# A planned attention-then-mixer kernel: the first pair's squares on ACT, the third group's squares planned later, by-token products spread among MLP tiles

## The chip, the cores and the metric

One core of one Trainium2 chip runs the whole program. The metric is the device time in microseconds (us). In the rounds here every timed run lies within 0.3% of its kernel's median; every comparison is of runs made in turn on the same chip. Engines: PE is the tensor engine, ACT the scalar engine, DVE the vector engine, POOL is GpSimd, SP the sync engine.

## The reference, cut to what matters

```python
# q, k, v: (8, 12, 448, 64) float32; U: (448, 32); V: (32, 448); w_ch1: (768, 3072); w_ch2: (3072, 768)
def _attn_ref(q, k, v, tau):
    q_n = q / (norm(q, axis=-1) + 1e-6)
    k_n = k / (norm(k, axis=-1) + 1e-6)
    attn = softmax(q_n @ k_n.T / tau)
    return attn @ v

def _moe_ref(x, U, V, w_ch1, w_ch2):          # x: the attention output as (8, 448, 768)
    u = x + ((x.T @ U) @ V).T                 # the low-rank mixer over tokens
    return u + relu(u @ w_ch1) @ w_ch2        # the MLP
```

## The kernel before

Every instruction is an `Op`; a planner written in Python simulates the engines with estimated durations, fixes the order on every engine, and the kernel then issues that order. ACT, DVE and PE run their queues in the order fixed, so an instruction that waits holds all behind it: in the traces below ACT stood 1.14 us ahead of a waiting square with an exponential ready behind it (before, 10.62). A `prio` says which of several ready instructions an engine takes (small first), `hold` and `deps` say what must be done before.

Heads go in pairs (two heads), pairs' statistics in groups: the first group is pair 1, the second pair 2, the third pairs 3 and 4, the fourth pairs 5 and 6. For each pair: squares, sums, ln and exp for the norm, products to normalise the rows (`xn`), transposes on PE (`tp`), scores (`sc`), exponentials on ACT, products with attention's V (`av`).

```python
def squares(b, g, ld, ops, lo, ii, ss, pr, on, hold):
    for i in ii:                                   # 0 is q, 1 is k
        for a0 in range(0, g, G // 2):
            o = Op(on, ..., deps=[ops[i], *hold], acq=[sq], prio=pr + 0.2, fast=True)   # x * x
            red.append(plan.add(Op("DVE", ..., deps=[o], ...)))                         # reduce_sum
# ... (cut)
def stats_first(ld, ops):
    for i in range(2):
        done[i], up = scales(0, 0, 2, ld, ops, 0, (i,), inv, -1 - 0.1 * i, ("DVE", "ACT")[i])
# ... (cut)
def by_tokens(us, A, X):                           # batch 0: u = x + A V, six products
    for i in range(3):
        for c0, c1 in ((0, CH), (CH, C)):
            mm = Slot(r_mm, 1)                     # one of three PSUM buffers
            o = plan.add(Op("PE", ...matmul(mm, V_sb[...], A[:, c0:c1])), pe_mlp)
            plan.add(Op("DVE", ...tensor_add(us[i][:, c0:c1], mm, X[:, i, c0:c1]), deps=[o], rel=[mm, X]))
# ... (cut)
for f in range(NC):                                # mlp: 24 tiles of relu(u @ w_ch1)
    if b == 0 and f == 9:
        by_tokens(us, *state["first"])
# ... (cut)
z = fill(lambda: nc.vector.memset(V_sb, 0.0), 500, prio=-1.3)
first = ...                                        # loads of q, k of pair 1, by SP
second = load_qk(0, 2, 4, uses=2)                  # the other loads, by POOL
ld, ops, _ = load_qk(0, 4, 8)
id_set = plan.add(Op("POOL", 0.8, lambda: make_identity(nc, ident)), pool_q)
begun = stats_first(*first[:2])
stats(0, 2, 4, *second, hold=begun)
zf = fill(lambda: nc.vector.memset(U_f(), 0.0), 400, prio=0.1, acq=[uv], deps=begun)
u0, v0, u1 = ...                                   # loads of the mixer's U and V, by SP, behind zf
stats(0, 4, 8, ld, ops, 0, hold=got[0, 0, "qkT"][2])   # third group: behind the copies of pair 1's transposes
load_v0()                                          # attention's V of batch 0, eight loads by POOL
ld, ops, _ = load_qk(0, 8, 12)
late = stats(0, 8, 12, ld, ops, 0)                 # fourth group
# ... (cut)
consts = [POOL cast of U, POOL cast of V into V_sb, POOL cast of U]
```

Of the kernel before, what the change touches and what calls it, by code (L numbers as in the profile page):

```python
# [49 lines left out]
class Plan:  # L50
# [52 lines left out]
    def run(self):  # L103
# [22 lines left out]
        while left:  # L126
# [6 lines left out]
            while progress:  # L133
                progress = False
                for e in self.ENGINES:
                    if free[e] > t + 1e-9:
                        continue
                    pick = None
                    if e in heads:
                        for k, s in enumerate(self.streams[e]):  # L140
                            i = heads[e][k]
                            if i < len(s):
                                r = self.ready_at(s[i], e)
                                if r is None:
                                    continue
                                if r <= t + 1e-9:
                                    pick = s[i]
                                    heads[e][k] += 1
                                    break
                                heapq.heappush(events, r)  # L150
                    else:
                        w = known[e]
                        for i, (_, _, o) in enumerate(w):
                            if o.start is not None:
                                continue
                            if e == "ACT" and o.fast and free["DVE"] <= t + 1e-9:
                                continue
                            r = self.ready_at(o, e)
                            if r is None:
                                continue  # L160
                            if r <= t + 1e-9:
                                pick = o
                                break
                            heapq.heappush(events, r)
                            if r <= t + self.HOLD:
                                break
                        if pick is not None:
                            del w[i]
                    if pick is None:
                        continue  # L170
                    o = pick
                    o.start, o.by = t, e
                    o.end = t + (o.dur[e] if isinstance(o.dur, dict) else o.dur)
                    free[e] = o.end
                    o.end += self.LAG[e]
                    if isinstance(o.lat, tuple):
                        q, work, fixed = o.lat
                        dma[q] = max(dma[q], o.end) + work
                        o.end = dma[q] + fixed
                    else:  # L180
                        o.end += o.lat
                    for s in o.acq:
                        if s.i is None:
                            s.i = s.ring.n
                            s.ring.n += 1
                    for s in o.rel:
                        s.left -= 1
                        s.last = max(s.last, o.end)
                        if s.left == 0:
                            s.ring.freed[s.i] = s.last  # L190
                    for c in kids.pop(o.seq, ()):
                        waits[c.seq] -= 1
                        if waits[c.seq] == 0:
                            offer(c)
                    order.append(o)
                    left -= 1
                    progress = True
                    heapq.heappush(events, free[e])
                    heapq.heappush(events, o.end + self.SEM)
# [5 lines left out]
def kernel(  # L205
# [12 lines left out]
    nc = tc.nc  # L218
# [276 lines left out]
    def stats_first(ld, ops):  # L495

        inv = Slot(r_inv, 3)
        done, ups = {}, []
        for i in range(2):
            done[i], up = scales(0, 0, 2, ld, ops, 0, (i,), inv, -1 - 0.1 * i, ("DVE", "ACT")[i])  # L500
            ups.append(up)
        return ups + norm(0, 0, ld, 0, inv, 0, done, -1)

# [58 lines left out]
    def attention(b, p, X):  # L562
# [4 lines left out]
        for m in (0, 1, 2, 6, 3, 4, 5) if b == 0 else range(7):  # L567
            sc = Slot(r_sc, 1)

            def score(sc=sc, m=m):  # L570
# [7 lines left out]
                out=attn.tile[:, m, off:off + S], in_=sc.tile[:, 0:S], func=AF.Exp,  # L578
                scale=inv_tau), deps=[o], acq=[attn], rel=[sc], prio=0.1 if b == 0 else 1))
        last_exp[b] = exps[5]  # L580
        muls = []
        for hh in range(2):
            h = 2 * p + hh
# [138 lines left out]
        prev["A"], prev["X"] = A, X  # L722
        return us, uT, ut

    def by_tokens(us, A, X):

        for i in range(3):
            for c0, c1 in ((0, CH), (CH, C)):
                mm = Slot(r_mm, 1)
                o = plan.add(Op("PE", pe_t(CH), lambda i=i, c0=c0, c1=c1, mm=mm: nc.tensor.matmul(  # L730
                    out=mm.tile[:, 0:CH], lhsT=V_sb[:, PAD + 128 * i:PAD + 128 * i + 128],
                    rhs=A.tile[:, c0:c1], start=True, stop=True), acq=[mm, us[i]], rel=[A]), pe_mlp)
                got.setdefault((0, "u"), []).append(plan.add(Op(
                    "DVE", dve_t(CH), lambda i=i, c0=c0, c1=c1, mm=mm: nc.vector.tensor_add(  # L734
                        out=us[i].tile[:, c0:c1], in0=mm.tile[:, 0:CH], in1=X.tile[:, i, c0:c1]),
                    deps=[o], rel=[mm, X], prio=2)))


    def mlp(b, us, uT, ut):
# [28 lines left out]
        for f in range(NC):  # L768
            if f % AHEAD == 0:
                for g in range(f, f + AHEAD):  # L770
                    early[g] = Slot(r_sc if b == 0 and f == 0 else r_mm, 1)
                    if f == 0 and b == 0:
                        up(g, early[g], range(CC - 1))
            if b == 0 and f == 9:
                by_tokens(us, *state["first"])
            mm = early[f]
            o = up(f, mm, range(CC - 1, CC) if b == 0 and f < AHEAD else range(CC))
            r = Op("ACT/DVE", any_t(n), None, deps=[o], acq=[relu], rel=[mm],
# [65 lines left out]
        nc.vector.memset(t_[96:128, :, 0:PAD].bitcast(mybir.dt.uint32), ones)  # L844

    attn_set = [fill(lambda t_=t_: set_attn(t_), 1000, prio=i - 2.5) for i, t_ in enumerate(attn_t)]
    z = fill(lambda: nc.vector.memset(V_sb, 0.0), 500, prio=-1.3)

    def load_u(par):
        off = PAD * par  # L850
# [25 lines left out]
    state, last_mul = {}, []  # L876

    def att(b):
        X = Slot(r_X, 0)
        muls = []  # L880
        for p in range(NPAIR):
            muls += attention(b, p, X)
        last_mul.extend(muls)
        return stage0(b, X, muls)
# [2 lines left out]
        out=lead.tile[:, i], in_=src[0, 0:2].rearrange("h (s c) d -> s h (c d)", c=SC)),  # L887
        acq=[uv], prio=-5, lat=2.5)) for i, src in enumerate((q, k))]
    second = load_qk(0, 2, 4, uses=2)
    ld, ops, _ = load_qk(0, 4, 8)  # L890
    id_set = plan.add(Op("POOL", 0.8, lambda: make_identity(nc, ident)), pool_q)
    begun = stats_first(*first[:2])
    stats(0, 2, 4, *second, hold=begun)
    xn_set.append(fill(lambda: nc.vector.memset(xn_t[2][:, 0:8, :], 0.0), 900, prio=0.2, deps=begun))
    zf = fill(lambda: nc.vector.memset(U_f(), 0.0), 400, prio=0.1, acq=[uv], deps=begun)
    u0 = load_u(0)
    v0 = [plan.add(Op("SP", 0.45, lambda t=t: nc.sync.dma_start(out=V_f()[R * t:R * (t + 1)], in_=moe_V),
                      deps=[zf, *begun], prio=-2, lat=12.0)) for t in range(4)]
    u1 = load_u(1)
    stats(0, 4, 8, ld, ops, 0, hold=got[0, 0, "qkT"][2])  # L900
    load_v0()
    ld, ops, _ = load_qk(0, 8, 12)
    late = stats(0, 8, 12, ld, ops, 0)
    load_w1(0, 6)
    load_w1(6, 12)
    v_set = [fill(lambda: set_v(v_t[0]), 1000, prio=-1.4),
             fill(lambda: set_v(v_t[1]), 1000, prio=3, deps=late)]
    consts = [plan.add(Op("POOL", 0.4, lambda: cast_u(0), deps=u0 + [z], rel=[uv]), pool_q),
              plan.add(Op("POOL", 1.2, cast_v, deps=v0 + [z], rel=[uv]), pool_q),
              plan.add(Op("POOL", 0.4, lambda: cast_u(1), deps=u1 + [z], rel=[uv]), pool_q)]  # L910
# [67 lines left out]
```

## Time and profile before

| | before |
|---|---|
| time, median of three runs | 604.51 us (604.49 to 605.16) |
| span of the profiled run | 603.2 us |
| first transposes on PE | 7.62 us |
| first exponential on ACT | 11.16 us |
| attention's V landed for the first head | 14.61 us |
| transposes of the second pair | 15.39 us |
| first scores of the third pair | 22.27 us |
| first full MLP tile | 41.29 us |

Times of events are from the span's start. In a timeline a line gives start, length, engine, line of the program, operation, tiles and count, and in brackets how long the engine had been idle and what ended that. The prediction below shows the lines that carry its argument. Two stretches matter later and are not in it. The first is DVE between 15 and 18 us, where before the copy of the second pair's transposed q stood in the midst of other work:

```profile
15.08 0.68 DVE L461 TENSOR_REDUCE ss<-sq 112x8 f32<-112x512 bf16 x1
16.36 0.75 DVE L826 COPY qkT<-tp 128x672 bf16<-128x672 bf16 x3 [0.60 <-PE tp L374]
17.03 0.68 DVE L461 TENSOR_REDUCE ss<-sq 112x8 f32<-112x512 bf16 x1
```

DVE waited 0.60 us for PE there. A table by stretch gives start and end, length, busy time of PE, weight loads, DVE, ACT and POOL with counts, then PE's clock, the DMA share and GB/s.

```profile
21.20:24.60 3.40, 1.99 (x18) 1.04 (x15) 3.30 (x11) 3.40 (x12) 1.16 (x1) 1.00 1.28 213
```

PE is busy for 1.99 of 3.40 us here.

One caution on every clock shown below, and in the prediction's table. The clock records of a trace begin late, here at 17.77 us, and the views show 1.00 for all that comes earlier. The products tell otherwise. The eight transposes at 15.39 (0.94 us, in the prediction) are 93 to 94 ns apart from start to start after the second (the first two 75), those at 19.79 are 48 to 51 ns apart:

```profile
19.79 0.56 PE L374 MATMUL tp<-ident,xn 112*128 112x112 bf16 x8
```

So PE ran at about half its clock at 15.39. A clock share below tells only of a fall after the first record.

### The profile page before, as it was taken

What the parts mean: (1) busy time and instruction counts of PE and PEld (TensorE: products, weight loads), DVE (VectorE), ACT (ScalarE), POOL (GpSimd) and SP (SyncE); (2) the same over time, 40 slices, a digit from 0 to 9 for tenths busy, and PEclk for the clock granted to TensorE, in tenths of its full rate; (3) what the DMA queues carried; (4) which work ended last, traced back from release to release, by engine and by line L of the source; (5) the groups of instructions that cost most, each with busy time, mean ns of one, the idle gap of its engine ahead of it and who ended that gap; (6) DMA issues with size and microseconds to landing.
All of it is one profiled execution on the core that took longest, in us unless ns stands there. A gap on an engine that the chain in (4) does not pass through costs nothing.

```text
span 603.2 us, 11528 instructions
## 1 busy us (share of the span) xinstructions
PE 586.4 (97%) x4725; PEld 347.0 (58%) x4725; DVE 300.6 (50%) x728; ACT 276.9 (46%) x598; POOL 115.2 (19%) x175
## 2 busy tenths in 40 slices
PE   3899999999999999999999999999999999999997
PEld 1565666555565665666445666566545666654565
DVE  8979749989999988554731244014300210110011
ACT  5877652488874277316741067505642025014300
POOL 8246334062706116000600000000000000000000
PEclk9999999999999999999999999999999999999999
DMA  9999999999999959725922133030002110310021
GB/s 144 193 188 112 204 201 107 150 173 136 159 152 155 149 102 154 95 57 90 123 29 66 52 74 47 1 93 27 15 1 53 52 40 1 90 42 1 0 53 54
DMA packets 150165, 54.81 MB, mean 91 GB/s; under 512 B 115040, under 2 KB 150112, under 8 KB 150112
## 3 DMA queue, kind: packets, MB, share of 16 engines
q0 software_dynamic: 72864, 25.73, 38.4%
q1 hardware_dynamic: 77184, 28.32, 24.4%
q8 instruction: 37, 0.61, 0.4%
q14 instruction: 16, 0.13, 0.1%
q10 hardware_dynamic: 64, 0.02, 0.0%
HBM read 52.25 MB, written 11.01 MB: 105 GB/s over the span
## 4 chain that ended last, share of the span: by engine, by line
PE 93%; DVE 2%; ACT 2%; POOL 1%; DMA 1%; issue 0%; ACTq 0%; POOLq 0%
PE mm L794 36%; PE mm L760 35%; PE sc L572 10%; PE av L592 8%; PE mm L684 1%; PE tp L374 1%; DMA v_nat<-in_v_dram 1%; DVE xn L536 1%; PE mm L649 1%; POOL v_nat L429 1%; ACT attn L577 1%; PE sc L760 0%; POOL qk_nat L396 0%; DVE ss L461 0%; ACT qkT L824 0%
## 5 line engine op out<-in xcount | busy, mean ns | idle before, releaser
L760 PE MATMUL mm<-uT,w_sb 128*128 128x512 bf16 (+1 forms) x1134 | 241.3, 353 | 0.2 <-DVE u_nat L734 0.2
L794 PE MATMUL mm<-w_sb,relu 128*128 128x384 bf16 (+1 forms) x1368 | 231.3, 323 | 0.0
L577 ACT ACTIVATE attn<-sc 128x448 bf16<-128x448 f32 x336 | 164.6, 552 | 110.9 <-PE av L592 58.2
L794 PEld LDWEIGHTS <-relu 128*128 128x128 bf16 x1368 | 132.7, 98 | 86.1 <-issue 0.2
L760 PEld LDWEIGHTS <-w_sb 128*128 128x128 bf16 x1152 | 111.8, 98 | 102.7 <-issue 1.8
L783 ACT ACTIVATE relu<-mm 128x512 bf16<-128x512 f32 (+1 forms) x158 | 86.8, 549 | 129.3 <-PE mm L760 128.7
L803 DVE TENSOR_TENSOR O_sb<-mm,u_nat 128x384 f32<-128x384 f32 (+1 forms) x57 | 31.2, 549 | 210.8 <-PE mm L794 207.4
L572 PE MATMUL sc<-qkT 128*128 128x448 bf16 x336 | 102.7, 356 | 3.7 <-ACT attn L577 2.0
L592 PEld LDWEIGHTS <-attn 128*128 128x128 bf16 x1536 | 62.1, 98 | 17.8 <-issue 2.5
L418 POOL DMA_DIRECT2D v_nat<-in_v_dram x98 | 63.2, 655 | 31.7 <-DMA w_sb<-in_moe_w_ch_dram 15.8
L592 PE MATMUL av<-v_nat,attn 128*128 128x65 bf16 x1536 | 66.6, 194 | 0.8 <-DMA v_nat<-in_v_dram 0.4
L461 DVE TENSOR_REDUCE ss<-sq 112x8 f32<-112x512 bf16 x96 | 63.1, 673 | 0.2
L536 DVE TENSOR_TENSOR xn<-qk_nat,inv 112x512 bf16<-112x512 bf16 x94 | 60.9, 681 | 2.4 <-DMA qkT<-xn 2.2
L396 POOL DMA_DIRECT2D qk_nat<-in_q_dram x24 | 17.2, 718 | 136.5 <-DVE xn L536 117.0
L572 PEld LDWEIGHTS <-qkT 128*128 128x128 bf16 x336 | 28.9, 98 | 22.1 <-issue 7.3
L601 DVE TENSOR_TENSOR X_sb<-av,rd 128x256 bf16<-128x256 f32 x96 | 40.1, 419 | 1.6
L599 DVE RECIPROCAL rd<-av 128x4 f32<-128x4 f32 x96 | 17.1, 179 | 37.6 <-PE av L592 36.9
L457 DVE TENSOR_TENSOR sq<-qk_nat 112x512 bf16<-112x512 bf16 x87 | 33.7, 415 | 0.0
L698 DVE TENSOR_TENSOR u_nat<-mm,X_sb 128x384 bf16<-128x384 f32 x36 | 19.2, 553 | 15.4 <-PE mm L684 15.1
L785 DVE TENSOR_SCALAR relu<-mm 128x384 bf16<-128x384 f32 (+1 forms) x31 | 18.7, 604 | 12.8 <-PE mm L760 12.0
L374 PE MATMUL tp<-ident,xn 112*128 112x112 bf16 x144 | 11.9, 226 | 7.8 <-DVE xn L536 7.6
L474 ACT ACTIVATE ln<-ss 112x32 f32<-112x32 f32 (+2 forms) x26 | 6.0, 231 | 27.3 <-DVE ss L461 27.1
(61 smaller groups left out, 172.5 us busy)
## 6 DMA issues: line engine op xcount, KB each, us to landing
qk_nat<-in_q_dram POOLq DMA_DIRECT2D x23, 224.0 KB, 5.2
qk_nat<-in_k_dram POOLq DMA_DIRECT2D x23, 224.0 KB, 6.3
w_sb<-in_moe_w_ch_dram POOLq DMA_DIRECT2D x4, 1152.0 KB, 14.6
w_sb<-in_moe_w_ch_dram POOLq DMA_DIRECT2D x8, 576.0 KB, 15.8
out_dram<-O_sb SPq DMA_DIRECT2D x15, 168.0 KB, 2.2
out_dram<-O_sb SPq DMA_DIRECT2D x16, 144.0 KB, 2.1
out_dram<-O_sb SPq DMA_DIRECT2D x16, 120.0 KB, 2.0
out_dram<-O_sb SPq DMA_DIRECT2D x16, 96.0 KB, 2.2
```

Of the source, the lines that this page charges most:

```text
L418: nc.gpsimd.dma_start(out=vb[p0:p0 + s1 - s0, hs, j, 0:D], in_=v[b, hs].rearrange("h (s c) d -> c s h d", c=SC)[c, s0:s1]),
L457: nc.vector.tensor_mul(y, x, x)
L461: lambda i=i, a0=a0, a1=a1, sq=sq: nc.vector.reduce_sum(ss.tile[:, i, a0:a1, :].rearrange("p h c -> p (h c)"), sq.tile[:, 0:a1 - a0, :].re ...
L536: nc.vector.tensor_mul(dst, src, sc)
L572: nc.tensor.matmul(out=sc.tile[:, 0:S], lhsT=kT[:, 128 * m:128 * (m + 1)], rhs=qkT.tile[:, 8:12, :].rearrange("p c s -> p (c s)"), start=T ...
L577: exps[m] = plan.add(Op("ACT", act_t(S), lambda sc=sc, m=m: nc.scalar.activation(out=attn.tile[:, m, off:off + S], in_=sc.tile[:, 0:S], fu ...
L592: nc.tensor.matmul(out=av.tile[:, t, 0:D + 1], lhsT=attn.tile[:, m, 128 * t:128 * (t + 1)], rhs=v_t[b % 2][:, h, j, 0:D + 1], start=(j == ...
L601: muls.append(plan.add(Op("DVE", dve_t(256), lambda av=av, rd=rd, h=h: nc.vector.tensor_mul(X.tile[:, :, h * D:(h + 1) * D], av.tile[:, :, ...
L760: o = plan.add(Op("PE", pe_t(n), lambda cc=cc: nc.tensor.matmul(out=mm.tile[:, 0:n], lhsT=w1_sb[:, cc, f * 128:(f + 1) * 128], rhs=uT.tile ...
L783: nc.scalar.activation(out=relu.tile[:, f, 0:n], in_=mm.tile[:, 0:n], func=AF.Relu)
L794: nc.tensor.matmul(out=mm.tile[:, 0:c1 - c0], lhsT=relu.tile[:, f, i * 128:(i + 1) * 128], rhs=w2_t[:, f, c0:c1], start=(f == 0), stop=(f ...
L803: nc.vector.tensor_add(out=O.tile[:, 0:w], in0=mm.tile[:, 0:w], in1=us[i].tile[:, c0:c1]),
```

## The change

The intent: start the first pair sooner by giving both of its squares to ACT, which is free (idle 2.26 us ahead of its first square in the trace before), and clearing the mixer's `V_sb` later; let the first exponentials run before the third group's squares; and spread the six by-token products of batch 0, which hold PE behind each other's adds, one by one among MLP tiles.

```diff
-                            if e == "ACT" and o.fast and free["DVE"] <= t + 1e-9:
+                            if e == "ACT" and o.fast and "/" in o.eng and free["DVE"] <= t + 1e-9:
-            done[i], up = scales(0, 0, 2, ld, ops, 0, (i,), inv, -1 - 0.1 * i, ("DVE", "ACT")[i])
+            done[i], up = scales(0, 0, 2, ld, ops, 0, (i,), inv, -1 - 0.1 * i, "ACT")
+        if b == 0 and p == 0:
+            last_exp["first"] = [exps[1]]
-    def by_tokens(us, A, X):
+    def by_tokens(us, A, X, part):
     ... (cut: one product per call)
-            if b == 0 and f == 9:
-                by_tokens(us, *state["first"])
+            if b == 0 and 9 <= f < 21 and f % 2:
+                by_tokens(us, *state["first"], (f - 9) // 2)
-    z = fill(lambda: nc.vector.memset(V_sb, 0.0), 500, prio=-1.3)
+    z = fill(lambda: nc.vector.memset(V_sb, 0.0), 500, prio=3, deps=begun)
+    muls0 = attention(0, 0, X0)                      # pair 1 entered into the plan here
-    stats(0, 4, 8, ld, ops, 0, hold=got[0, 0, "qkT"][2])
+    stats(0, 4, 8, *third, hold=last_exp["first"])
     ... (cut: the same loads entered earlier, in the same order on POOL)
```

More of the change, by code (lines that the diff above doesn't have):

```diff
@@ L723, in stage0 @@
         return us, uT, ut
-    def by_tokens(us, A, X):
-        for i in range(3):
-            for c0, c1 in ((0, CH), (CH, C)):
+    def by_tokens(us, A, X, part):
+        for i in range(part // 2, part // 2 + 1):
+            for c0, c1 in [((0, CH), (CH, C))[part % 2]]:
                 mm = Slot(r_mm, 1)
@@ L878, in att @@
     def att(b):
-        X = Slot(r_X, 0)
-        muls = []
-        for p in range(NPAIR):
+        X = Slot(r_X, 0) if b else X0
+        muls = [] if b else list(muls0)
+        for p in range(0 if b else 1, NPAIR):
             muls += attention(b, p, X)
@@ L889 @@
     second = load_qk(0, 2, 4, uses=2)
-    ld, ops, _ = load_qk(0, 4, 8)
+    third = load_qk(0, 4, 8)
     id_set = plan.add(Op("POOL", 0.8, lambda: make_identity(nc, ident)), pool_q)
-    begun = stats_first(*first[:2])
+    load_v0()
+    fourth = load_qk(0, 8, 12)
+    v_set = [fill(lambda: set_v(v_t[0]), 1000, prio=-1.4)]
+    begun = stats_first(*first)
+    X0 = Slot(r_X, 0)
+    muls0 = attention(0, 0, X0)
     stats(0, 2, 4, *second, hold=begun)
     xn_set.append(fill(lambda: nc.vector.memset(xn_t[2][:, 0:8, :], 0.0), 900, prio=0.2, deps=begun))
+    z = fill(lambda: nc.vector.memset(V_sb, 0.0), 500, prio=3, deps=begun)
     zf = fill(lambda: nc.vector.memset(U_f(), 0.0), 400, prio=0.1, acq=[uv], deps=begun)
@@ L899 @@
     u1 = load_u(1)
-    stats(0, 4, 8, ld, ops, 0, hold=got[0, 0, "qkT"][2])
-    load_v0()
-    ld, ops, _ = load_qk(0, 8, 12)
-    late = stats(0, 8, 12, ld, ops, 0)
+    stats(0, 4, 8, *third, hold=last_exp["first"])
+    late = stats(0, 8, 12, *fourth)
     load_w1(0, 6)
     load_w1(6, 12)
-    v_set = [fill(lambda: set_v(v_t[0]), 1000, prio=-1.4),
-             fill(lambda: set_v(v_t[1]), 1000, prio=3, deps=late)]
+    v_set.append(fill(lambda: set_v(v_t[1]), 1000, prio=3, deps=late))
     consts = [plan.add(Op("POOL", 0.4, lambda: cast_u(0), deps=u0 + [z], rel=[uv]), pool_q),
```

## The prediction

> **What bounds the kernel now.** I read the page's engine shares and its slices first, then a table of busy time by stretch, the waits of the tensor engine, the chain that ended last, and the timelines of the first 62 us.
>
> ```profile
> PE 586.4 (97%) x4725; PEld 347.0 (58%) x4725; DVE 300.6 (50%) x728; ACT 276.9 (46%) x598; POOL 115.2 (19%) x175
> ```
>
> ```profile
> PE tp L374 <- DVE xn L536: 7.6, 1, 7.6
> PE sc L572 <- ACT attn L577: 2.0, 4, 1.0
> ```
>
> ```profile
> 0.00:15.00 15.00, 5.51 (x29) 2.46 (x30) 13.11 (x39) 8.82 (x22) 12.74 (x22) 1.00 1.38 144
> 15.00:30.00 15.00, 12.40 (x151) 8.55 (x149) 13.95 (x42) 13.27 (x36) 4.22 (x6) 1.00 1.15 194
> 30.00:45.00 15.00, 14.59 (x194) 9.54 (x193) 11.30 (x32) 11.01 (x28) 6.96 (x11) 1.00 1.19 187
> 45.00:60.00 15.00, 14.22 (x116) 8.74 (x114) 14.06 (x29) 11.01 (x25) 9.82 (x15) 1.00 1.22 113
> ```
>
> The second fence is who PE waited for, us in total, times and longest; in the third the first number after a stretch's length is PE's busy time. PE is the bound: 97% of the span. It is idle 9.5 us of the first 15 us, 2.6 of the next 15, 0.4 and 0.8 after that, and in the table hardly at all from 60 us until the drain. So the change cannot remove matmul work; it can only remove PE's holes in the first 60 us, and 2% (12.1 us) is nearly all of the 13.3 us of idle in that stretch, 7.6 of which are the wait for the first data. That rules out large gains.
>
> The chain that ended last, in order of time (start, length, what), gives what ends those holes:
>
> ```profile
> 5.11 4.37 POOL v_nat L429 x6
> 9.48 5.13 DMA v_nat<-in_v_dram
> 14.65 0.93 PE av L592 x14
> 18.57 0.98 ACT attn L577 x2
> ```
>
> It runs through the load of V, not through the squares: V's last piece for the first head lands at 9.48 + 5.13 = 14.61, and the first attention-times-V products go on at 14.65. (This V is attention's, `v_nat`; the mixer's small V, `V_sb`, is another tensor.) More pieces, from the timelines of PE, ACT and DVE in turn:
>
> ```profile
> 14.33 1.25 PE L592 MATMUL av<-v_nat,attn 128*128 128x65 bf16 x15 [0.44 <-DMA v_nat<-in_v_dram]
> 15.39 0.94 PE L374 MATMUL tp<-ident,xn 112*128 112x112 bf16 x8
> ...
> 22.27 0.35 PE L572 MATMUL sc<-qkT 128*128 128x448 bf16 x1 [0.78 <-ACT qkT L824]
> ...
> 50.01 1.17 PE L730 MATMUL mm<-A_sb,V_sb 128*128 128x384 bf16 x3
> ...
> 52.39 0.79 PE L730 MATMUL mm<-A_sb,V_sb 128*128 128x384 bf16 x2 [0.24 <-DVE u_nat L734]
> ...
> 53.91 0.81 PE L760 MATMUL mm<-uT,w_sb 128*128 128x384 bf16 x4 [0.19 <-DVE u_nat L734]
> ```
>
> ```profile
> 10.62 0.63 ACT L455 ACTIVATE sq<-qk_nat 112x512 bf16<-112x512 bf16 x1 [1.14 <-DVE ss L461]
> 11.16 0.53 ACT L577 ACTIVATE attn<-sc 128x448 bf16<-128x448 f32 x1
> ```
>
> ```profile
> 18.99 1.88 DVE L536 TENSOR_TENSOR xn<-qk_nat,inv 112x512 bf16<-112x512 bf16 x3
> ```
>
> The reader should see: the transposes of the second pair (15.39) stand right behind the V products; the first exponential is late (11.16) because a square of the third group stands before it on ACT and waits for a buffer; the third group's normalised rows start at 18.99 and its first scores at 22.27; and the by-token products of batch 0 (L730) stop PE from 50.01 to 53.91.
>
> [...] 11 matmuls of L760 from 55.46 to the next start at 57.24 are 162 ns each. Busy time hides small stalls, so I count start to start. [...] ACT held a ready exponential 1.14 us behind a waiting square. [...] the trace has 0.63 for one square and 1.13 for two. [...] V's 168 KB pieces took 5.9 us to land in the median. [...] it is why V is late.
>
> **The change part by part.**
>
> (a) Fill of the mixer's V later and both first squares on ACT. Before, DVE clears `V_sb` (4.12, 0.30 us), squares q at 4.34 and reduces from 5.00, though q landed 2.9 us after its issue at 0.74, at 3.64. Now ACT squares q at about 3.66 to 4.29 and k when it lands (1.18 + 3.1 = 4.28) to 4.91; DVE reduces q from 4.33. Everything behind moves up by 5.00 - 4.33 = 0.67 us: first transposes at 6.95 instead of 7.62, first scores at 8.75.
>
> (b) The third group's first ACT square now stands behind the fifth exponential. The first exponential then starts at about 9.35 (scores at 8.75 + 0.6) instead of 11.16. But ACT's next instruction is the logarithm of the second group, which needs two reductions that end near 10.5, so the seventh exponential ends near 14.0 instead of 15.02: 1.0 us. The second group's normalised rows, 13.88 to 15.16 before, end near 13.7.
>
> (c) What (a) and (b) buy then meets V. PE's stream still has the first head's 16 V products before the second pair's transposes. V's loads are issued by the same POOL queue at the same times, so the products finish near 15.3 and the transposes start at 15.33 instead of 15.39. Of 1.0 to 1.5 us gained, about 0.1 is kept.
>
> (d) The new order makes two engines wait there. On DVE the copy of the second pair's transposed q now stands *before* most of the third group's squares and reductions; it cannot run before the transposes end, near 17.0, so DVE, done with its earlier work at 14.9, idles 2.1 us. ACT likewise holds the copy of the keys (16.35 to 17.4) before its second square of the third group. From 18.0 DVE still has, start to start: four reductions (0.61 each), two squares (0.34), scalar work 0.1 + 0.4, one multiply 0.38, that is 4.0 us, so the third group's rows start at 22.0 instead of 18.99; four normalisations follow to 24.4, then the q copy, and the third pair's first scores come at about 24.8 instead of 22.27. PE has done other work meanwhile (14 more V products, 0.4 us; four transposes, 0.2). ACT restarts its exponentials near 25.5 with 28 of them at 0.457 us (19 took 8.89 with 0.2 of gap), one key copy 0.95 and 0.2 of small work: until 39.5, where before the last ended at 37.85. That would cost 1.6 us. ACT had 0.6 us of idle in this stretch that may close, and PE has slack of its own, so I take +1.2.
>
> (e) The by-token products. From 50.01 to 53.91 PE did 6 of them at 0.162, 5 scores at 0.189 and 8 transposes at 0.050: 2.3 us of work in 3.9. The stall is 1.58 us, because with three PSUM buffers each product waits for an add on DVE (0.5 us, behind reductions of 0.65). Spread over six odd MLP tiles of 6 x 0.162 = 0.97 us, a buffer has 1.9 us to come free. I take back 1.4 and leave 0.2 for new short waits. PE is bound from there on, so this reaches the end whole.
>
> Sum: -0.1 + 1.2 - 1.4 = -0.3, from 604.5 to 604.2.
>
> **Rivals.** *The front gains too* (602 to 603): if PE and ACT make up all of (d), the by-token part alone gives 603.1, and an earlier first stage something more. For it: ACT is idle 2.3 us before 18. Against: V's landing is on the chain, and POOL's issues are not moved. *The front loses in full and the spread products stall* (605 to 606): each now holds one of three buffers while DVE works on batch 1, so relu tiles could wait; against it, 1.9 us is more than an add behind two reductions (0.5 + 1.3). *A transfer becomes the bound*: if PE reaches the MLP earlier it might wait for weights; against it, PE waited for no weight load before, and a shift of 1 to 2 us is small. *Hidden in the noise*: the three times lie within 0.7 us, so a net of 0.3 cannot be told from none.
>
> **Range and chances.** The two parts have about ±1.2 us each, so 602.3 to 606.0 around 604.2. Either 2% limit is ten microseconds away from anything I can construct: 1% each.
>
> **What would show it.** (a) first transposes at about 6.95. (b) first exponential near 9.4. (c) V products still at 14.3 to 15.3, waiting for the V load. (d) DVE idle near 15 to 17 before the q copy, third group's rows near 22, third pair's scores near 24.8, last exponential of batch 0 after 38.5. (e) No wait of PE for the by-token adds between 50 and 75 us. I am wrong if V lands earlier or PE does not wait for it, if the third pair's scores start before 23, or if PE shows new holes among the MLP tiles.

## The result, and the profile after

The changed kernel took **606.12 us** in the median (605.99 to 606.41, four runs) against 604.84 for the kernel before on the same chip (604.49 to 605.16). A ratio here is the mean time of one kernel's runs over the mean of the other's runs of the same rounds, so not quite the ratio of the medians: it is 1.0022, 95% interval 1.0005 to 1.0039. That is within 2%, as given the best chance, but 0.1 us above the predicted range, and the sign of the difference is the opposite of the predicted one.

Page, shares and PE's clock by slices of 1/40 of the span:

```profile
PE 588.1 (97%) x4725; PEld 348.0 (58%) x4725; DVE 300.6 (50%) x726; ACT 277.3 (46%) x600; POOL 114.2 (19%) x175
...
PEclk9899999999999999999999999999999999999999
```

PE is busy 1.7 us longer with the same number of matmuls, and the second slice has an 8. Timeline of PE:

```profile
6.93 1.50 PE L374 MATMUL tp<-ident,xn 112*128 112x112 bf16 x12 [6.93 <-DVE xn L536]
...
15.27 1.19 PE L594 MATMUL av<-v_nat,attn 128*128 128x65 bf16 x14 [1.29 <-DMA v_nat<-in_v_dram]
16.27 0.94 PE L374 MATMUL tp<-ident,xn 112*128 112x112 bf16 x8
...
22.64 0.68 PE L594 MATMUL av<-v_nat,attn 128*128 128x65 bf16 x16 [1.15 <-DVE X_sb L603]
23.24 2.51 PE L374 MATMUL tp<-ident,xn 112*128 112x112 bf16 x24
25.54 1.33 PE L572 MATMUL sc<-qkT 128*128 128x448 bf16 x3
...
43.46 2.44 PE L762 MATMUL sc<-uT,w_sb 128*128 128x384 bf16 x14 [0.24 <-ACT uT L826]
...
56.75 0.33 PE L732 MATMUL mm<-A_sb,V_sb 128*128 128x384 bf16 x1
```

The first transposes came 0.69 us sooner; the third pair's first scores 3.27 us later, the first full MLP tile 2.17 us later (43.46 against 41.29). The by-token products (L732) stand alone among MLP tiles and no wait for an add precedes them. ACT and DVE in the same trace:

```profile
9.28 0.55 ACT L577 ACTIVATE attn<-sc 128x448 bf16<-128x448 f32 x1 [0.53 <-PE sc L572]
...
17.24 1.03 ACT L826 COPY qkT<-tp 128x672 bf16<-128x672 bf16 x3 [3.32 <-PE tp L374]
```

```profile
13.61 1.27 DVE L461 TENSOR_REDUCE ss<-sq 112x8 f32<-112x512 bf16 x2
18.00 0.39 DVE L828 COPY qkT<-tp 128x448 bf16<-128x448 bf16 x1 [3.12 <-PE tp L374]
...
22.50 2.48 DVE L536 TENSOR_TENSOR xn<-qk_nat,inv 112x512 bf16<-112x512 bf16 x4
```

Both engines stand idle for over 3 us behind the second pair's transposes, which stand behind V. The table by stretch:

```profile
20.40:23.80 3.40, 2.00 (x27) 1.06 (x25) 3.40 (x10) 2.51 (x7) 0.98 (x1) 1.00 1.27 209
23.80:27.20 3.40, 3.32 (x30) 2.41 (x30) 3.35 (x10) 2.82 (x10) 0.74 (x2) 0.50 1.21 213
```

PE falls back to **half its clock for 3.4 us**, just when the third pair's transposes come: 24 of them took 2.3 us start to start, the first eight 49 to 60 ns apart, those after 23.84 mostly 92 to 94.

The sum of it: from trace to trace the first MLP tile moves by +2.17. The waits of PE from 50 to 65 us, counted start to start beyond the pace of each shape, fall from 2.07 to 0.90, so -1.17. Later the rest is +0.06. That makes +1.06 at the last matmul (599.51 to 600.57), as the spans do (603.2 to 604.2).

### The profile page after: what moved, and what is told of

Same layout as the page of the kernel before. It is cut to its first block, busy times and chain, and to the rows that moved or that the text cites. A ratio compares the mean times of both kernels' runs of the same rounds, so it can differ in the third digit from the quotient of the medians. Undisturbed runs are those within 1.5% of the kernel's fastest.

```text
span 604.2 us, 11535 instructions
## 1 busy us (share of the span) xinstructions
PE 588.1 (97%) x4725; PEld 348.0 (58%) x4725; DVE 300.6 (50%) x726; ACT 277.3 (46%) x600; POOL 114.2 (19%) x175
## 3 DMA queue, kind: packets, MB, share of 16 engines
q1 hardware_dynamic: 77184, 28.32, 24.8%
## 4 chain that ended last, share of the span: by engine, by line
PE 91%; DVE 3%; ACT 2%; DMA 2%; issue 0%; POOL 0%; ACTq 0%; POOLq 0%
PE mm L796 35%; PE mm L762 34%; PE sc L572 10%; PE av L594 8%; ACT attn L577 1%; PE mm L686 1%; PE tp L374 1%; DMA qk_nat<-in_q_dram 1%; DVE ss L461 1%; DMA v_nat<-in_v_dram 1%; PE mm L651 1%; DVE sq L457 1%; PE sc L762 0%; DVE xn L536 0%; DVE u_nat L700 0%
## 6 DMA issues: line engine op xcount, KB each, us to landing
w_sb<-in_moe_w_ch_dram POOLq DMA_DIRECT2D x8, 576.0 KB, 15.9
```

## The experiments

All times are medians; "ratio" is to the kernel before in the same rounds, which had medians of 605.71 (first four), 605.18 (e5 to e8), 605.33 (e9 to e12), 605.39 (e13 to e16) and 605.36 (last two). "Clock" is the mean granted clock of each timed run; in these rounds the kernel before has 0.999 or 1.000 in 48 of 51 runs and 0.997 in three. The last three columns are from each profiled execution: V landed (the seventh of its eight loads; in the trace after 9.99 + 5.55 in the chain that ended last), first scores of the third pair, first full MLP tile. Two faulty runs, e9_ulate and e11_both, are told below and not listed.

| run | time | ratio (95%) | clock | V | scores | MLP |
|---|---|---|---|---|---|---|
| before | 604.84 | 1 | 1.000 | 14.61 | 22.27 | 41.29 |
| after | 606.12 | 1.0022 (1.0005 to 1.0039) | 0.993 to 0.997 | 15.54 | 25.54 | 43.46 |
| e1_tokens | 604.42 | 0.9984 (0.9970 to 0.9998) | 1.000, one 0.997 | 14.41 | 22.07 | 41.59 |
| e2_front | 607.50 | 1.0029 (1.0016 to 1.0042) | 0.994 to 0.997 | 15.01 | 25.03 | 42.90 |
| e3_vfill | 606.21 | 1.0015 (1.0002 to 1.0029) | 0.993 to 0.997 | 15.28 | 26.05 | 44.41 |
| e4_vlate | 606.60 | 1.0020 (1.0005 to 1.0036) | 0.994 to 1.000 | 15.70 | 24.00 | 42.17 |
| e5_fill | 604.54 | 0.9988 (0.9976 to 1.0000) | 0.999 to 1.000 | 15.93 | 24.10 | 42.13 |
| e6_warm | 605.48 | 1.0003 (0.9991 to 1.0015) | 0.999 to 1.000 | 14.38 | 24.97 | 42.70 |
| e7_pool | 606.07 | 1.0009 (0.9997 to 1.0022) | 0.994 to 0.997 | 14.59 | 25.35 | 43.53 |
| e8_hold | 606.04 | 1.0012 (0.9999 to 1.0026) | 0.999 to 1.000, one 0.997 | 15.54 | 24.78 | 42.55 |
| e10_again | 606.48 | 1.0016 (1.0004 to 1.0028) | 0.994 to 0.997 | 15.08 | 25.86 | 44.03 |
| e12_sq | 606.44 | 1.0015 (1.0003 to 1.0027) | 0.994 to 1.000 | 15.55 | 26.14 | 44.32 |
| e13_fillpool | 605.30 | 0.9999 (0.9987 to 1.0012) | 1.000 | 15.34 | 24.86 | 42.83 |
| e14_pool2 | 606.25 | 1.0010 (0.9996 to 1.0023) | 0.993 to 0.997 | 15.62 | 26.07 | 43.92 |
| e15_ulate2 | 605.18 | 0.9998 (0.9984 to 1.0012) | 0.994 to 1.000 | 14.78 | 24.86 | 42.78 |
| e16_fill2 | 604.71 | 0.9985 (0.9973 to 0.9998) | 0.999 to 1.000 | 14.56 | 24.04 | 42.10 |
| e17_tokfrozen | 605.99 | 1.0014 (1.0000 to 1.0028) | 0.997 to 1.000 | 14.79 | 22.54 | 41.92 |
| e18_cast | 605.80 | 1.0008 (0.9995 to 1.0020) | 0.994 to 0.997 | 15.18 | 25.02 | 43.43 |

**The theories.** Main: the new order on ACT and DVE leaves both idle behind the second pair's transposes, and these behind V, so the third group comes late. Rivals: V lands late by itself; the early squares or the later clear of `V_sb` do harm elsewhere; PE's half clock is the loss; the by-token part does not gain.

### The two halves of the change, each alone

`e1_tokens` is the kernel before with only the by-token part; `e2_front` is the changed kernel with the six products together again at tile 9:

```diff
-            if b == 0 and 9 <= f < 21 and f % 2:
-                by_tokens(us, *state["first"], (f - 9) // 2)
+            if b == 0 and f == 9:
+                for part in range(6):
+                    by_tokens(us, *state["first"], part)
```

> The kernel before with the by-token part of the change alone (one product per odd MLP tile). Theory: the two parts add up; the PE stall of 1.58 us at 50 to 54 us goes, and the time falls by 1.2 us (0.9 to 1.5) to about 603.6, the first MLP tile staying at 41.3. Rival: the gain seen in the changed kernel's 50 to 75 us is only slack moved about, so the time stays within 0.4 us of before.

> The changed kernel with the by-token products together again at the tenth tile. Theory: the front alone costs what the first MLP tile shows (43.46 against 41.29 in the two traces), 2.2 us: about 607.0, and 1.2 us above the changed kernel. Rival: the front costs only the 1.3 us of the whole, and the by-token part does nothing: about 606.1.

The by-token part alone gains 0.0016 of 605.7, or 1.0 us; the front alone loses 0.0029, or 1.8 us. So the by-token rival falls, and the loss lies in the front. PE's waits from 50 to 65 us fall by 1.3 in e1_tokens (2.07 to 0.77). Part of it is lost again near 103 us, where the planner made a new order. Waits of PE, total, times and longest, in e1_tokens:

```profile
PE tp L374 <- DVE O_sb L803: 0.7, 1, 0.7
```

### Undoing the parts of the early start

`e3_vfill` clears `V_sb` where the kernel before does. `e12_sq`, with the planned order frozen, gives the square of the first q back to DVE ahead of the first reduction.

```diff
-    z = fill(lambda: nc.vector.memset(V_sb, 0.0), 500, prio=3, deps=begun)
+    z = fill(lambda: nc.vector.memset(V_sb, 0.0), 500, prio=-1.3)          # e3_vfill
```

```diff
+    lead_q.by = "DVE"                                                      # e12_sq
+    order.remove(lead_q); order.insert(order.index(lead_red[0]), lead_q)
```

> The changed kernel with the clear of the mixer's V at its old place, ahead of the first reduction. Theory for the later landing of attention's V (15.54 against 14.61): its loads start 0.4 us earlier on POOL because DVE no longer clears beside POOL's identity, and collide with the third group's loads; then V lands near 14.6 again and the time falls by about 0.9 us to 605.2. Rival: one DMA engine of the profiled run lagged, or the U loads that start 0.7 us earlier are the cause; then V's landing does not follow this edit, and the time stays at 606.1 or rises by 0.1 to 0.2.

> The changed kernel, order frozen, with the square of the first q given back to DVE in its old place ahead of the first reduction. First transposes go from 6.93 back to 7.5 to 7.6 and U's loads start near 9.0. If the whole gain of the early start is lost behind V's landing, as predicted, the first MLP tile does not move later: V lands at 14.4 to 15.0 as in the kernel before and the time stays within 0.4 of the changed kernel, or is up to 0.6 better. If the early start was worth its 0.67, the first MLP tile and the time are 0.4 to 0.7 later.

Neither brings anything: ratios 1.0015 and 1.0015, V at 15.28 and 15.55 (14.4 to 15.0 was expected of e12_sq). In e12_sq the first transposes come at 7.30 instead of 6.93 and the time is that of the changed kernel beside it (606.44 and 606.48). No help or harm of the early start is seen; an effect below some 0.7 us, the half width of these intervals, could hide.

### The order

`e4_vlate` lets the planner believe that V lands 3 us later (one argument, `late=5.0`), so that it puts the second pair's transposes ahead of the V products.

> The changed kernel with attention's V planned to land 3 us later, which moves the second pair's 12 transposes and three of its scores ahead of the first products with V on PE, and little else. Theory: PE's in-order wait for V is what held the transposes (16.27) and, behind the copies of them, the third group's work on DVE and ACT; then the transposes run near 13.7, the third group's rows come near 20 and the first MLP tile near 41, and the time falls by 2 to 3 us to 603.1 to 604.1, below the kernel before. Rival: the third group is late because its squares are planned late, whatever V does; then the rows stay near 22 and the time within 0.7 us of 606.1.

The transposes came at 13.25 and the first MLP tile at 42.17, 1.29 sooner. But the time stayed (606.60, ratio 1.0020): the planner made the order anew everywhere, PE's waits from 70 to 150 us rose from 2.25 to 4.67, and DVE met another wait:

```profile
16.91 0.42 DVE L457 TENSOR_TENSOR sq<-qk_nat 112x512 bf16<-112x512 bf16 x1 [1.63 <-DMA qk_nat<-in_q_dram]
```

So a change of the plan's inputs is no clean experiment here. `e5_fill` keeps the changed kernel's planned order and moves nine instructions in it: the third group's last square, its ln and exp, two of its reductions, its add and reciprocal and the products of its first pair now stand ahead of the copies that wait for V. `e16_fill2` is the same kernel once more, on the chip of e10_again.

```diff
     order = plan.run()
+    acts = [o for o in order if o.by == "ACT"]
+    dves = [o for o in order if o.by == "DVE"]
+    early = [dves[29], acts[20], dves[33], acts[23], acts[25], dves[38], dves[40], dves[42], dves[43]]
+    at = acts[19]                                   # the copy of the second pair's keys
+    order = [o for o in order if o not in early]
+    i = order.index(at)
+    order[i:i] = early
```

> The changed kernel with its planned order frozen; only nine instructions move: the third group's last square (ACT), two reductions, ln, exp, the add, the reciprocal and the two products of its first pair's rows (DVE) now stand ahead of the copies of the second pair's transposes, where ACT stood idle 3.32 us and DVE 3.12 us. Main theory (the static order leaves both engines idle behind the late V): third group's rows ready near 18 instead of 22.50, third pair's first scores near 23.5 to 24 instead of 25.54, first MLP tile near 41.8 instead of 43.46, and about 1.2 us off the time against the changed kernel. If the half clock at 23.8 to 27.2 alone is the cause, the clock falls all the same and the first MLP tile moves by less than 0.4. If the late V alone is the cause, the first MLP tile stays within 0.4 of 43.46 too.

> e5_fill itself again, as the base for e13_fillpool on the same chip and as a second trace of it: 604.4 to 604.7, clock 0.999 to 1.0 in every run, V at 15 to 16, third pair's first scores near 24.1, first MLP tile near 42.1.

Timeline of DVE in e5_fill:

```profile
13.62 2.06 DVE L461 TENSOR_REDUCE ss<-sq 112x8 f32<-112x512 bf16 x3
16.23 0.18 DVE L480 TENSOR_SCALAR ln<-ln 112x32 f32<-112x32 f32 x1 [0.56 <-ACT ln L477]
...
16.84 1.29 DVE L536 TENSOR_TENSOR xn<-qk_nat,inv 112x512 bf16<-112x512 bf16 x2
18.38 0.39 DVE L828 COPY qkT<-tp 128x448 bf16<-128x448 bf16 x1 [0.25 <-PE tp L374]
```

PE in e5_fill, then in e16_fill2:

```profile
15.96 0.88 PE L594 MATMUL av<-v_nat,attn 128*128 128x65 bf16 x13 [0.17 <-DMA v_nat<-in_v_dram]
...
22.59 1.59 PE L374 MATMUL tp<-ident,xn 112*128 112x112 bf16 x24
24.10 0.74 PE L572 MATMUL sc<-qkT 128*128 128x448 bf16 x3
...
42.13 2.44 PE L762 MATMUL sc<-uT,w_sb 128*128 128x384 bf16 x14 [0.24 <-ACT uT L826]
```

```profile
14.30 1.16 PE L594 MATMUL av<-v_nat,attn 128*128 128x65 bf16 x14 [1.04 <-DMA v_nat<-in_v_dram]
...
42.10 2.44 PE L762 MATMUL sc<-uT,w_sb 128*128 128x384 bf16 x14 [0.24 <-ACT uT L826]
```

DVE's idle of 3.12 us shrinks to 0.56 and 0.25, the third group's first rows start at 16.84 instead of 22.50, the 24 transposes take 1.5 us, the clock, once full, does not fall again in any of the ten timed runs, and the time falls below the kernel before, twice: ratios 0.9988 and 0.9985. On the same chip the changed kernel has 1.0016 (1.0004 to 1.0028), and the intervals do not meet. That is 0.0031, or 1.9 us. **The order is the cause.** And V, 15.93 in one and 14.56 in the other, moves the first MLP tile by 0.03: with this order its landing sets nothing.

The traces show what the order does: it ties the third group to V. In all ten traces with the changed front as planned (after, e2, e3, e6, e7, e10, e12, e14, e15, e18) the third group's rows start 6.95 to 6.97 us after V lands; in the three with the front of before (before, e1, e17) it is 4.38 or 4.39. So in those orders a later V moves the rows by as much, and the rival of the late V is not apart from the order: it costs through it. In e5_fill and e16_fill2 the rows start at 16.84 and 17.12, whenever V lands.

The third pair's scores are still 1.8 us later than before (24.1 and 22.27). PE had the second pair's first V products ahead of the third pair's transposes, and they began at 22.07 behind DVE's product `X_sb` (21.60), which stands behind fourth-group squares and reductions. This rest was not tried.

`e8_hold` undoes only the hold (third group's squares behind pair 1's copies, as before) and lets the planner make the order anew:

```diff
+    turned = got[0, 0, "qkT"][2]                    # ahead of attention(0, 0, X0)
-    stats(0, 4, 8, *third, hold=last_exp["first"])
+    stats(0, 4, 8, *third, hold=turned)
```

> The changed kernel with the third group's squares held as in the kernel before, behind the copies of the first pair's transposes instead of behind its second exp. The planner makes a new order from that. If the hold is what put these squares behind the copies that wait for V, third group's rows come at 18 to 20 instead of 22.50 and the first MLP tile at 41.5 to 42.5; if V's landing or the clock are all, the first MLP tile stays at 43.2 to 43.7. Either way the order further on is made anew and can move the time by up to 1 us in either direction.

The first MLP tile came 0.9 sooner (42.55), just past the upper end of what was expected, and the rows at 21.11, where 18 to 20 was expected: a part of what the main theory says, no more. PE's waits from 70 to 150 us rose by 1.5 and the time stayed (606.04), which shows again what a new order costs.

### The half clock

`e6_warm` puts 21 spare products of the identity on PE where it waits for `X_sb`, ahead of the second pair's V products; the order is otherwise kept.

```diff
     for o in order:
+        if o is last_exp["av1"]:
+            for z in range(21):
+                if z % 7 == 0:
+                    warm = psum.tile([128, 512], FP, name="mm", tag="mm", bufs=3)
+                nc.tensor.matmul(out=warm[:, 0:128], lhsT=ident, rhs=ident, start=True, stop=True)
```

> The changed kernel, order kept, with 21 spare 128x128 products of the identity put on PE just ahead of the second pair's value products, where PE waits 1.15 us for the copy of the first pair's outputs. They take some 1.2 us of time in which PE has nothing. Theory of the half clock: PE too idle from 20.4 to 23.8 costs it half its clock from 23.8 to 27.2; with the spare products it keeps 1.0, the 24 transposes that took 2.3 us take about 1.3, third pair's first scores come at 24.5 to 24.7, and the first MLP tile 0.5 to 1.0 earlier than 43.46. If the order on ACT and DVE is all, the clock stays up but the first MLP tile stays within 0.3, or is later by the spare products' time.

```profile
19.00:22.40 3.40, 3.04 (x47) 2.27 (x46) 3.40 (x9) 2.75 (x7) 0.61 (x1) 1.00 1.27 216
22.40:25.80 3.40, 2.21 (x24) 1.25 (x22) 3.40 (x8) 2.16 (x8) 0.46 (x1) 1.00 1.23 211
```

The clock stayed at 0.999 to 1.000 in all five timed runs, where the changed kernel had 0.993 to 0.997 in all nine of its own (after and e10_again). The first MLP tile came at 42.70. The fairest partner is e7_pool of the same rounds, with the same order, V at 14.59 against 14.38 and equally slow products (below): its clock was 0.50 from 22.5 to 29.3, two stretches of 3.4 us, and its first MLP tile came at 43.53. Of these 0.83 us V's later landing has 0.20 (rows at 21.54 against 21.34); some 0.6 is left for two stretches, so about **0.3 us** for the one of the trace after. This is an estimate from one pair of traces. In the timed runs e6_warm is 0.4 us below e7_pool (1.0003 against 1.0009) and about 0.8 to 1.1 us below the changed kernel (1.0016 to 1.0022), though all these intervals overlap. The timed runs of the changed order sort alike: in after, e7, e10, e14 and e18 the 15 runs with a clock of 0.996 or 0.997 lie 0.65 us above the mean of the kernel before in their rounds, the nine with 0.993 or 0.994 lie 0.95 above it, and single runs scatter by some 0.5.

What makes the clock fall is not shown. PE was far from idle ahead of it: busy 2.00 of the 3.40 us before the fall in the trace after (20.40 to 23.80), 1.85 in e2_front (19.40 to 22.80), 1.80 in e4_vlate (19.90 to 23.30). In e6_warm, with the spare products, 3.04 us (19.00 to 22.40) and then 2.21 (22.40 to 25.80) brought no fall. But 1.99 us in the trace before (21.20 to 24.60) brought none either, and in e7_pool 2.59 us of work at half clock (22.50 to 25.90) was followed by 3.40 us more of it. So PE's busy time in such a stretch does not by itself tell the two apart, and no limit can be read from these traces.

### Why V's landing came out differently

V landed at 15.54 in the trace after, not at the predicted 14.61. Three readings were tried. First, V's loads were issued earlier (4.68 instead of 5.06), as POOL's last step on the identity took 0.29 us instead of 0.69. In the trace before that step (4.42 to 5.11) ran beside the fp32 square on DVE (4.34 to 4.96); in e12_sq, where the square (4.03 to 4.65) met only its start (4.45), it took 0.35. `e7_pool` and `e14_pool2` put a spare clear on POOL behind the identity (128x256 and 128x512), and `e13_fillpool` does so with e5_fill's order.

```diff
+    def wait_identity():
+        make_identity(nc, ident)
+        nc.gpsimd.memset(idle_t, 0.0)
-    id_set = plan.add(Op("POOL", 0.8, lambda: make_identity(nc, ident)), pool_q)
+    id_set = plan.add(Op("POOL", 0.8, wait_identity), pool_q)
```

> The changed kernel, plan kept, with one spare clear of 128x256 on POOL behind the identity, so that V's loads are issued some 0.2 to 0.4 us later, about where the kernel before has them (5.06 instead of 4.68). If the early issue of V's loads is what made V land at 15.54 (its seventh and eighth loads wait for the third group's loads, whose landing it delays), V lands at 14.4 to 15.0 and the first MLP tile comes 0.4 to 0.9 earlier than 43.46. If not, V lands at 15.5 to 15.9 and the first MLP tile stays or is 0.3 later.

> The changed kernel with the same spare clear on POOL, twice that of e7_pool. If the early issue of V's loads is what makes V late, V lands at 14.4 to 14.7 again, third group's k by 10.0; with the half clock still there the first MLP tile comes at 43.0 to 43.6 and the time gains no more than 0.3 on 606.2 (as e7_pool, 606.07). If not, V at 15.0 to 16.0.

> The rearranged order of e5_fill with a spare clear of 128x512 on POOL behind the identity, so that V's loads are issued near 5.2 instead of 4.67. If the early issue is what makes V late: V at 14.4 to 14.7, first MLP tile at 41.2 to 41.7 instead of 42.14, time 0.4 to 0.8 below e16_fill2 of the same rounds, 603.7 to 604.2. If not: V at 15.0 to 16.0, first MLP tile at 42.0 to 42.6, time within 0.2 of e16_fill2.

e7_pool seemed to confirm it (V at 14.59), but e14_pool2 and e13_fillpool, issued later still (5.13 and 5.14), had V at 15.62 and 15.34, and e6_warm with the early issue had 14.38. The reading falls.

Second, U's loads start sooner. `e9_ulate` and `e11_both` (the same with e5_fill's order) moved the clear that these loads wait for.

```diff
+    order.remove(zf)
+    order.insert(adds[2], zf)                       # the loads themselves were left where they stood
```

> The changed kernel, order frozen; only the clear of the buffer that the loads of U wait for moves from 8.08 to about 11.2 us on DVE, so that these loads start near 11.4 instead of 8.38. In the ten traces so far V's landing went with the start of U's loads (8.38 to 8.54: V at 15.3 to 15.9; 8.65 to 9.12: 14.4 to 15.0). If U's loads take the share of the transfers that V needs, V now lands by 14.6 and third group's k by 9.9, with the first transposes still near 7.0. If it only goes along with something earlier (how soon the first q and k came in), V still lands at 15.3 or later when the first transposes come before 7.1. Time: 0.3 to 0.7 below the changed kernel of the same rounds under the first, within 0.3 under the second.

> The rearranged order of e5_fill and the later loads of U of e9_ulate together. If both causes are real, V by 14.6, third pair's first scores near 23, first MLP tile near 41.2 to 41.5, clock 0.999 to 1.0, time 603.8 to 604.3 and 0.9 to 1.5 below the kernel before of the same rounds. If U's loads don't matter: as e5_fill, 604.4 to 604.6.

Both were faulty. The loads stayed ahead of the clear in program order, so they started at 1.67 and the clear then wiped what they had brought: the results were wrong (relative error 0.48), and nothing is taken from them. `e15_ulate2` moves the clear and its loads together.

```diff
+    late_u = sorted([zf, *u0, *v0, *u1], key=order.index)
+    order = [o for o in order if o not in late_u]
+    order[adds[2]:adds[2]] = late_u
```

> The repair of e9_ulate: the clear of U's buffer and all loads behind it move together, so that U's loads start near 11.4 instead of 8.38, and the result is right. If U's loads take V's share: V by 14.7 although its loads are issued at 4.67. If the early issue of V's loads is the cause: V at 15.0 to 15.9 all the same, and the time within 0.3 of 606.2, or worse if U itself comes too late.

U's loads started at 11.20, V landed at 14.78, just outside the 14.7 expected if U were the cause, and the time fell to 605.18, where e14_pool2 in the same rounds had 606.25; those intervals overlap. That leans to U's loads, but e16_fill2 had V at 14.56 with U's loads at 8.67.

Third, chance: `e10_again` is the changed kernel unaltered.

> The changed kernel itself once more, on the same chip as the three beside it, as the base for them and to see how far one trace stands for all. Expected 605.9 to 606.4, granted clock 0.993 to 0.997 in every run; V lands anywhere from 14.4 to 15.9, later the sooner the first transposes come; first MLP tile 43 to 43.7.

V at 15.08 with one trace, 15.54 with the other (and the first MLP tile at 44.03, past the 43.7 expected); and e5_fill and e16_fill2, one kernel, are 1.37 us apart. In every trace of a right kernel V lands 4.2 to 5.4 us after the third group's k (4.9 in before, 4.6 in after), and k's own landing moves as much. Over the changed front V lands anywhere from 14.4 to 15.9; the kernel before has one trace and e1_tokens and e17_tokfrozen, with its front, one each (14.61, 14.41, 14.79). So one landing time for such a load says little: e5_fill and e16_fill2 issued V's first load at 4.67 and 4.68, yet in e5_fill the seventh and eighth stood 0.80 and 0.63 us behind the third group's q and k, and in e16_fill2 neither did. What decides it within an execution **stays open**.

### Why an earlier V did not help in e7_pool

In the unrepaired order V at 14.59 (e7_pool) brought the first MLP tile no sooner than V at 15.54 (43.53 and 43.46). DVE and POOL in e7_pool:

```profile
21.54 3.26 DVE L537 TENSOR_TENSOR xn<-qk_nat,inv 112x512 bf16<-112x512 bf16 x4
...
22.13 1.52 POOL L867 CAST V_sb<-raw_uv 128x448 bf16<-128x448 f32 x1 [6.14 <-DMA raw_uv<-in_moe_U_dram]
```

The third group's rows started 0.96 us sooner than in the trace after (21.54 and 22.50), but the four products took 3.26 instead of 2.48, one of them 1.47 us where the median is 0.68: they met POOL's cast of the mixer's V. And the half clock came for two stretches instead of one. Side by side both took longer here (the cast 1.52 us, where it took 0.98 in the trace after, ahead of the products but for 0.06 us); in e17_tokfrozen the product alone did (1.36 us, the cast 0.98), in the trace before the cast alone (1.16, the product 0.69). The four products took 3.28 us in e6_warm, 3.27 in e10_again, 3.00 in e12_sq and 2.87 in e14_pool2, where the cast ran into them, and 2.58 in e15_ulate2, where it came after them (24.95); in e5_fill the cast (20.70 for 0.98 us) ran beside two reductions, which took 1.27 us together, as they did without it in the trace before (1.27 from 9.91); in e13_fillpool, with POOL half a microsecond behind, it began at 21.63 and the two products took 1.91 instead of 1.29. That fits its being 0.6 us slower than e16_fill2, but so does its clock, which by the records was first full at 24.30 instead of 21.68; the two are not told apart. `e18_cast` lets the cast change places with the second cast of U.

```diff
+    order.remove(consts[1])
+    order.insert(order.index(consts[2]) + 1, consts[1])
```

> The changed kernel, order frozen; on POOL the cast of moe_V changes places with the second cast of U, so that it comes at 25 us or later instead of near 22, when third group's rows are being made. If the cast slows DVE's products of these rows, the four take 2.4 to 2.6 us in all instead of 2.9 to 3.3, the first MLP tile comes at 42.6 to 43.3, earlier for an earlier V, and the time is 0.3 to 0.7 below that of the changed kernel: ratio to before 1.0005 to 1.0012 instead of 1.0016 to 1.0022. If the slowing has another cause, 2.9 to 3.3 us can still come and the ratio stays.

```profile
22.14 2.48 DVE L536 TENSOR_TENSOR xn<-qk_nat,inv 112x512 bf16<-112x512 bf16 x4
...
27.27 3.39 DVE L536 TENSOR_TENSOR xn<-qk_nat,inv 112x512 bf16<-112x512 bf16 x4
```

The third group's products took 2.48 and the third pair's scores came at 25.02, 2.88 after the rows; in e3, e7 and e10, where cast and products met at the same half clock, it was 3.81 to 3.82, in after, e2 and e15, where they did not, 3.04 to 3.12. So the collision was the cause of the length, and costs some 0.7 to 0.8 us there. But the cast, moved to 28.07, met the fourth group's products instead, which took 3.39. The ratio was 1.0008, inside what was expected; the first MLP tile was at 43.43, later than expected, with the half clock from 24.3 to 27.8 as well. What the collision is worth in the time is not shown.

### The part that gains, alone, in a frozen order

`e17_tokfrozen` keeps the kernel before's planned order and only moves five of the six by-token products to tiles 11 to 19, and their adds behind those tiles' copies.

```diff
+    for k in range(1, 6):
+        first, relu_f = tile_at[9 + 2 * k]          # first product and copy of that tile
+        ... (cut)
+        order.insert(i, tok[k])                     # i: place of that first product
+        order.insert(order.index(relu_f) + 1, got[0, "u"][k])
```

> The kernel before with its planned order frozen; five of the six by-token products move among the MLP tiles 11 to 19 and their adds behind the copies of those tiles. The front stays as before (first MLP tile 41.0 to 41.8, clock 0.999 to 1.0). The by-token waits of 1.58 at 50 to 55 fall to some 0.3 to 0.5, and the 0.8 us that e1_tokens lost again near 103 does not come, as the order there is not made anew: 603.9 to 604.3 if the kernel before is at 605.4, ratio 0.997 to 0.9985. If the gain of e1_tokens hung on its own new order, the ratio is 0.999 to 1.000.

A miss: 605.99, ratio 1.0014. PE's waits from 50 to 65 us were 2.13, not less than the 2.07 of before. Moving the products without what stands around them gives new waits, for instance 0.25 us for an exponential at 53.76; the gain of e1_tokens needs the order that the planner made for it. The first MLP tile too was 0.63 later than in the trace before (41.92), of which V, at 14.79, has 0.18. So the versions that beat both kernels are e1_tokens and e5_fill, by about 0.15% of the kernel before, each with an interval that touches or stays just below 1.

## Why the prediction was wrong, point by point

- **The bound and its limits** held: PE busy 97%, nothing but holes of the first 65 us moved, far within 2%.
- **(a)** held: first transposes at 6.93 (6.95 predicted). e12_sq shows that this start is worth nothing at the end, as (c) argued.
- **(b)** held: first exponential at 9.28 (9.35 predicted).
- **(c) is the step that failed.** It let V land as before, at 14.61, so that the second pair's transposes start at 15.33 and 0.1 is kept. V's loads were not issued at the same times but 0.38 sooner (4.68), and V landed at 15.54, the transposes started at 16.27: 0.88 lost where 0.1 gained was predicted. As the order of (d) ties the rows to V (22.50 is 6.96 after 15.54), the loss passes on whole. The step rested on one trace of something that differs by 1.37 us between two traces of one kernel (15.93 in e5_fill, 14.56 in e16_fill2). On average V landed at 15.10 in the ten traces of this order and at 14.60 in the three with the front of before, so a loss of 0.5 rather than 0.9 may be the rule.
- **(d)** had the mechanism right: DVE idle 3.12 us ahead of the q copy, rows at 22.50 (22.0 predicted), scores at 25.54 (24.8 predicted). Its size came out near, 2.17 - 0.88 = 1.29 against 1.2, but partly by luck. The rows came 6.96 after V where the prediction had 7.4 (22.0 - 14.61), and the fall to half the clock, some 0.3, was not considered at all. In the second trace of the same kernel, e10_again, the split is another: the transposes at 15.80 lose 0.41 and (d) 2.33 (44.03 - 41.29 - 0.41), with the cast in the way and two stretches at half clock. There (d) is the step that is too small. In both traces the front's net, +1.1 by the prediction, is the error; putting the order right (e5_fill, e16_fill2) takes away the wait for V and the fall of the clock together.
- **(e)** held nearly: -1.17 of PE's waits against -1.4 predicted, and 1.0 us in the time for the part alone.
- **The sum**, with the measured terms: 0.88 + 1.29 - 1.17 + 0.06 = +1.06 in the traces where -0.3 was predicted; the timed runs differ by 1.28 in the median, and where V landed in those is not on record. Of the rivals, "the front loses in full" came nearest, 605 to 606, though its spread products did not stall.

## What to carry to other kernels

A static order that puts an engine's copy behind a late transfer stops all that stands behind the copy (here DVE for 3.12 us, ACT for 3.32); look for work that is ready and move that ahead, in the frozen order, before touching what the planner is fed, for a new plan moved microseconds elsewhere here (PE's waits from 70 to 150 us rose by 2.4 in e4_vlate, by 1.5 in e8_hold). When PE is kept waiting, count the clock too: here a fall to half clock for 3.4 us cost, by estimate, some 0.3 us. And before a sum rests on the landing of a load, take more than one trace of it.
